# Batch 0's rows of v by one-hot matmuls in place of a gather, and the stores around the last gather in smaller parts, each waiting for one three or four places ahead

## The chip, the cores and the metric

The kernel runs on one core of a Trainium2 chip. The metric is the device time of one execution in microseconds (us), as the median of the runs shown. Engines are named as in the profile: PE (matmuls), DVE (vector), ACT (scalar), POOL (GpSimd, which here issues all loads, gathers and scatters on queue q0) and SP (which issues the stores on queue q1). Both queues are worked off by the same 16 DMA engines.

## What is computed

Four batches of q, k and v, each 6208 x 256 in float32. Attention runs across channels, so its matrix is 256 x 256, and a mixture-of-depths step then changes the 128 best rows of each batch:

```python
qn = q / (norm(q, axis=1) + 1e-06); kn = k / (norm(k, axis=1) + 1e-06)
s = kn.transpose(0, 2, 1) @ qn / tau
a = softmax(s)
x = v @ a                                   # (4, 6208, 256)
scores = x @ w_gate
for b in range(B):
    top_idx = the 128 rows with the highest scores[b]
    xe = x[b, top_idx]
    ye = np.maximum(xe @ w1, 0.0) @ w2      # w1 256 x 1024, w2 1024 x 256
    g = 1.0 / (1.0 + np.exp(-scores[b, top_idx]))
    out[b, top_idx] = xe + g[:, None] * ye
```

## The kernel before

A batch is cut into six chunks of 1024 rows and a rest of 64. A chunk's tile has 128 partitions with 8 rows each (RPP), so a full load moves 1 MB of float32 and casts it to 512 KB of bf16 on its way (emit_load, L187), and a store of a chunk sends 8 KB from each partition (emit_store, L514). The rest is a piece of its own and comes second in `order`.

For each batch the kernel goes through four stages. p1_row (L292) sums k'q and the squares of q and k on PE, row by row as the loads arrive. softmax_stages (L310) makes the 256 x 256 matrix a. p2_transpose (L392) turns v's tiles by PE into vt_sb, p2_score (L422) multiplies them with a's gate column for the scores, and p2_out (L456) multiplies them with a; ACT copies these outputs into a stage tile (L482). select_stages (L522) runs as a coroutine: seven rounds of compares and counts find the threshold (cmp, L557), a mask and its prefix counts give each chosen row its place (msk, pre), and idx, the 128 row numbers, follows (L622). Then POOL gathers the 128 rows of v from DRAM (L626) into vg; PE turns them (L637), DVE copies them to vgt (L639), and the small network runs on PE, ACT and DVE up to upd (L689). When the batch's stores have landed, POOL scatters upd over the output (L721).

The work is written out by a planner, while the program is built: a loop at the end of the kernel keeps a clock per engine (vt_clock) and a model of the two DMA queues (Rings), and at each step emits the ready piece of lowest priority number; each engine then runs its instructions in the order in which they were emitted. pump() issues the next load on POOL as soon as a buffer counts as free (in_use against limit) and fewer than four are in flight. out_store (L828) emits the stores on SP. Stores of batches 2 and 3 are deferred until the loads of the last batch are nearly done, and two chunks of batch 1 (`late`, with the change by the network applied in a matmul) go out last of all. SP and POOL work in order: a store or a load that waits holds all behind it.

```python
    QK_BUFS = 5
    V_BUFS = 5
    ST_BUFS = 9
    VT_BUFS = 11
...
        yield ("pool", 0.15, 0.9)
        vg = moe.tile([P, C], BF16, name="vg", bufs=2)
        ins = nc.gpsimd.indirect_dma_start(out=vg, out_offset=None, in_=v_flat,
                                     in_offset=bass.IndirectOffsetOnAxis(ap=idx[:, 0:1], axis=0))
```

Of the kernel before, what the change touches and what calls it, by code (L numbers as in the profile page):

```python
# [10 lines left out]
F32 = mybir.dt.float32  # L11
BF16 = mybir.dt.bfloat16
# [3 lines left out]
ALU = mybir.AluOpType  # L16
AX = mybir.AxisListType

P = 128
RPP = 8  # L20
CHUNK = RPP * P
NTHR = 8
# [5 lines left out]
def kernel(  # L28
# [12 lines left out]
    nc = tc.nc  # L41
# [13 lines left out]
    inv_tau = 1.0 / float(tau)  # L55

    QK_BUFS = 5
    V_BUFS = 5
    ST_BUFS = 9
    VT_BUFS = 11  # L60
    AHEAD = 4

    const = ctx.enter_context(tc.tile_pool(name="const", bufs=1))
# [88 lines left out]
    def now():  # L152
        return vt_clock["pe"]
# [110 lines left out]
    for i in range(NSTEP):  # L264
        nc.vector.memset(pows[:, i, :], 1.00001 / (NTHR + 1) ** (i + 1))
    jpows = const.tile([P, NSTEP, NTHR], F32)
    nc.vector.tensor_tensor(out=jpows, in0=pows,
                            in1=iota_row[:, None, 1:NTHR + 1].to_broadcast([P, NSTEP, NTHR]), op=ALU.mult)
    ones_col = const.tile([P, NCOL], BF16)
    nc.vector.memset(ones_col, 1.0)  # L270
    cnt9 = const.tile([P, NTHR + 1], F32)
# [219 lines left out]
    def emit_eights():  # L491
# [4 lines left out]
        for i in range(4):  # L496
# [3 lines left out]
            if i == 0:  # L500
# [2 lines left out]
                    mybir.DependencyInfo(mybir.DependencyClass.Sync, mybir.DependencyReason.DATA),  # L503
                    reason="stores behind loads")

    def emit_store(b, ci, parts):
        st = stage_of.pop((b, ci))
        ins = []
        keep = dmas if (b, ci) not in late else []
        if ci < NFULL:  # L510
            for h in range(parts):
                rows = slice(h * RPP // parts, (h + 1) * RPP // parts)
                low = slice(AHEAD_OF if (b, ci) == UNEVEN else 0, P)
                ins.append(nc.sync.dma_start(out=view(out, b, ci)[low, rows, :], in_=st[low, rows, :]))  # L514
        else:
            ins.append(nc.sync.dma_start(out=view(out, b, ci), in_=st[:REM, 0, :]))
        if (b, ci) not in late:
            held[b] -= 1
        keep.extend(ins)
        return ins[0]  # L520

    def select_stages(b):  # L522
        sc_ps = sc_tiles[b]
# [29 lines left out]
        nc.vector.tensor_scalar(out=tab, in0=jpows, scalar1=rng, scalar2=None, op0=ALU.mult)  # L553
        wait = 1.8
        for i in range(NSTEP):
            cmp = moe.tile([P, NCOL, NTHR], BF16, name="cmp", bufs=2)
            nc.vector.scalar_tensor_tensor(out=cmp, in0=sc[:, 0:NCOL, None].to_broadcast([P, NCOL, NTHR]),  # L557
                                           scalar=wl[:, i, NTHR:NTHR + 1],
                                           in1=tab[:, None, i, :].to_broadcast([P, NCOL, NTHR]),
# [39 lines left out]
        nc.tensor.matmul(sc_ps[:, 0, 0:1], lhsT=tri_b[:, 0, :], rhs=own_b, start=True, stop=True)  # L599
        excl_b = moe.tile([P, NCOL + 1], BF16, name="excl_b")  # L600
        nc.scalar.copy(excl_b, sc_ps[:, 0, 0:1].to_broadcast([P, NCOL + 1]))
        oh = moe.tile([P, P], BF16, name="oh")
        nc.vector.tensor_scalar(out=oh, in0=iota_row, scalar1=mps[:, 0:1], scalar2=None, op0=ALU.is_ge)
        nc.vector.scalar_tensor_tensor(out=oh, in0=iota_row, scalar=mps[:, 1:2], in1=oh, op0=ALU.is_lt,
# [13 lines left out]
        if b == late[0][0]:  # L618
# [2 lines left out]
        idx = moe.tile([P, 1], I32, name="idx", bufs=2)  # L621
        nc.vector.tensor_scalar(out=idx, in0=tok, scalar1=float(N - 1), scalar2=float(b * N), op0=ALU.min,  # L622
                                op1=ALU.add)
        yield ("pool", 0.15, 0.9)
        vg = moe.tile([P, C], BF16, name="vg", bufs=2)
        ins = nc.gpsimd.indirect_dma_start(out=vg, out_offset=None, in_=v_flat,  # L626
                                     in_offset=bass.IndirectOffsetOnAxis(ap=idx[:, 0:1], axis=0))
        dmas.append(ins)
        vt_clock["pool"] = max(vt_clock["pool"], now()) + 1.0
        rings.add(0, vt_clock["pool"] + 1.0, 0.5, ("gather", b))  # L630
        gathered.add(b)

        yield ("dma", ("gather", b))
        a_sb, _ = a_tiles[b]
        tp = ps_vt.tile([P, 2, 4, P], BF16, name="vt_ps")
        for cc in range(2):
            nc.tensor.transpose(tp[:, cc, 0, :], in_=vg[:, cc * P:(cc + 1) * P], identity=ident_b)  # L637
        vgt = moe.tile([P, 2, P], BF16, name="vgt")
        nc.vector.tensor_copy(vgt, tp[:, :, 0, :])  # L639
        yield ("pe", 0.12, 0.3)  # L640

        xt_ps = ps_vt.tile([P, 2, C], F32, name="vt_ps")
        for dc in range(2):
# [88 lines left out]
    def calm():  # L732

        if acc_dead[0]:
            return L in gathered
        if softmaxes[0]:
            return False
        near = eat[eat_at:eat_at + 14]
        return not any(x[0] == "T" for x in near) or near[0][0] == "T"

    class Chain:
# [33 lines left out]
        def ready(self):  # L775
            if self.need[0] == "t":
                if self.b == E and self.mlp and acc_dead[0] and L not in gathered:
                    return FAR
                return self.need[1]
            if self.need[0] == "dma":  # L780
# [12 lines left out]
            return max(rings.landing(key) for key in stored[b]) + 3.0  # L793
# [34 lines left out]
    def out_store(b, ci):  # L828
# [6 lines left out]
            gate = GATE  # L835
        if gate:
            vt_clock["sp"] = max(vt_clock["sp"], rings.landing(arrival_key[gate]))
        parts = 1 if ci == NFULL else 2 if b == L and ci in order[3:5] else 2 if 0 < len(gate_done) < 3 else 1
        if gate_done:
            gate_done.append(1)  # L840
        key = ("st", b, ci)
# [25 lines left out]
    while True:  # L867
# [106 lines left out]
        elif what == "T":  # L974
# [20 lines left out]
            vt_bank = sorted(vt_bank)[1:] + [fin]  # L995
            vt_live = len(from_pool)
            vt_ready[(u[1], g)] = fin
            if eat_at == len(eat) or eat[eat_at][1] != u:
                in_use[bucket(u)] -= 1
        elif what == "S":  # L1000
            b, g = scores[score_at]
# [61 lines left out]
```

## Time and profile before

| | us |
|---|---|
| median of 3 runs | 258.37 (258.06 to 258.6) |
| the profiled execution | 257.8 |
| its span | 255.8 |
| PE busy in the span | 214.7 |
| DVE busy | 92.6 |
| ACT busy | 106.4 |
| POOL busy | 56.9 |

The profile is that of one execution. Its span runs from the first to the last instruction; the execution's own time is 2.0 us longer. "Busy" of an engine is the time in which it ran an instruction. A DMA queue's share is the time that its packets took, as a share of 16 engines over the stretch; two queues can overlap, so that shares add up to a little over 100%. A strip shows the span (or a window) in 40 equal slices, each digit the busy share in tenths, 9 for 90% or more.

### The profile page before, as it was taken

The page shows a single profiled execution, that of the slowest core. Times are in us where ns is not written, and L with a number is a line of the kernel's source. Part 1 is how long each engine was busy: PE and PEld are TensorE (multiplying, and loading weights), DVE is VectorE, ACT ScalarE, POOL GpSimd, SP SyncE. Part 2 cuts the span into 40 slices and gives each one's busy share as a digit, 9 for nine tenths or more (in the row PEclk, how much of TensorE's full clock was granted, in tenths as well). Part 3 has the DMA queues.
Part 4 walks back from the last instruction along what each step waited for, and adds up shares of the span by engine and source line. Part 5 has one row for each costly group of instructions (what it writes and reads, how often), then busy time and mean ns, then how long its engine had stood idle before and what let it go on. Part 6 is the DMA issues. An engine that isn't in the chain of part 4 may idle for free.

```text
span 255.8 us, 6666 instructions
## 1 busy us (share of the span) xinstructions
PE 214.7 (84%) x2878; PEld 187.9 (73%) x2878; DVE 92.6 (36%) x410; ACT 106.4 (42%) x187; POOL 56.9 (22%) x106
## 2 busy tenths in 40 slices
PE   0099779899998529989999689899999999999962
PEld 0069768798877529879888578788898878887851
DVE  2000002635651003445655006546752064687021
ACT  2800003753564002484244005765313069698740
POOL 7323111422005000622200414212313310000301
PEclk9999999999999959999999999999999999999987
DMA  6999999999999999999999999999999999999995
GB/s 235 259 216 215 213 216 210 215 209 251 274 320 314 316 285 216 218 214 213 249 282 258 213 211 213 215 261 316 220 215 218 212 225 225 407 425 411 404 415 250
DMA packets 17326, 66.87 MB, mean 261 GB/s; under 512 B 2097, under 2 KB 3634, under 8 KB 14450
## 3 DMA queue, kind: packets, MB, share of 16 engines
q0 software_dynamic: 12672, 38.93, 76.5%
q1 hardware_dynamic: 4626, 27.53, 26.7%
q8 instruction: 22, 0.36, 0.5%
q14 instruction: 6, 0.05, 0.0%
HBM read 78.91 MB, written 25.95 MB: 410 GB/s over the span
## 4 chain that ended last, share of the span: by engine, by line
DMA 73%; PE 14%; issue 4%; POOL 4%; DVE 2%; ACT 1%; POOLq 1%; DVEq 0%
DMA k_ch<-in_k_dram 48%; DMA v_ch<-in_v_dram 10%; DMA q_ch<-in_q_dram 10%; DMA out_dram<-stage 4%; PE s_ps L303 2%; PE o_ps L474 2%; PE vt_ps L403 2%; POOL q_ch L187 1%; PE g_ps L307 1%; PE g_ps L305 1%; ACT stage L482 1%; PE s_ps L474 1%; PE sc_ps L440 1%; PE g_ps L474 1%; POOL k_ch L187 1%
## 5 line engine op out<-in xcount | busy, mean ns | idle before, releaser
L303 PE MATMUL s_ps<-q_ch,k_ch 128*128 128x256 bf16 x384 | 90.0, 279 | 28.7 <-DMA k_ch<-in_k_dram 28.7
L305 PE MATMUL g_ps<-q_ch 128*128 128x128 bf16 x384 | 85.5, 223 | 0.0
L307 PE MATMUL g_ps<-k_ch 128*128 128x128 bf16 x384 | 85.5, 223 | 0.0
L482 ACT COPY stage<-o_ps 128x512 f32<-128x512 f32 x77 | 43.9, 589 | 43.6 <-PE o_ps L474 41.6
L303 PEld LDWEIGHTS <-k_ch 128*128 128x128 bf16 x384 | 38.3, 100 | 31.5 <-DMA k_ch<-in_k_dram 30.6
L307 PEld LDWEIGHTS <-k_ch 128*128 128x128 bf16 x384 | 38.3, 100 | 5.2
L305 PEld LDWEIGHTS <-q_ch 128*128 128x128 bf16 x384 | 38.3, 100 | 0.1
L474 PE MATMUL o_ps<-a_sb,vt_sb 128*128 128x256 bf16 (+1 forms) x250 | 35.5, 272 | 1.0 <-ACT stage L482 0.5
L317 DVE CUSTOM_DVE_ANT_0 junk<-g_ps,ident_f 128x128 f32<-128x128 f32 x16 | 4.7, 291 | 66.4 <-PE g_ps L307 66.0
L474 PEld LDWEIGHTS <-vt_sb 128*128 128x128 bf16 (+1 forms) x264 | 23.6, 97 | 6.4 <-issue 3.1
L403 PE MATMUL vt_ps<-ident_b,v_ch 128*128 128x128 bf16 x360 | 25.4, 219 | 2.7 <-ACT vt_sb L417 2.4
L403 PEld LDWEIGHTS <-v_ch 128*128 128x128 bf16 x384 | 23.1, 97 | 5.1 <-issue 3.4
L313 ACT COPY s_sb<-s_ps 128x512 f32<-128x512 f32 x4 | 2.3, 586 | 55.4 <-PE s_ps L303 55.4
L187 POOL DMA_DIRECT2D v_ch<-in_v_dram x26 | 14.2, 545 | 45.8 <-PE vt_ps L403 17.5
L417 ACT COPY vt_sb<-vt_ps 128x1024 bf16<-128x1024 bf16 (+1 forms) x26 | 22.6, 927 | 2.9 <-PE vt_ps L403 2.9
L187 POOL DMA_DIRECT2D q_ch<-in_q_dram x25 | 13.8, 554 | 29.9 <-DMA q_ch<-in_q_dram 10.4
L187 POOL DMA_DIRECT2D k_ch<-in_k_dram x25 | 13.6, 543 | 24.5 <-DMA v_ch<-in_v_dram 10.4
L865 PE MATMUL o_ps<-w_sb,ident_b 128*128 128x256 bf16 x124 | 18.8, 273 | 0.2 <-ACT h_sb L675 0.2
L557 DVE SCALAR_TENSOR_TENSOR cmp<-sc,wl,tab 128x392 bf16<-128x392 f32 x28 | 17.5, 627 | 1.0
L626 POOL DMA_INDIRECT vg<-in_v_dram,idx x4 | 4.0, 1008 | 61.0 <-DVE idx L622 32.8
L865 PEld LDWEIGHTS <-ident_b 128*128 128x128 bf16 x124 | 10.7, 97 | 1.3 <-issue 0.4
L576 DVE TENSOR_REDUCE cnt<-m_ps 128x8 f32<-128x56 f32 x28 | 6.0, 216 | 15.3 <-PE m_ps L573 14.9
(188 smaller groups left out, 273.7 us busy)
## 6 DMA issues: line engine op xcount, KB each, us to landing
out_dram<-stage SPq DMA_DIRECT2D x21, 1024.0 KB, 10.2
q_ch<-in_q_dram POOLq DMA_DIRECT2D x23, 512.0 KB, 17.8
k_ch<-in_k_dram POOLq DMA_DIRECT2D x23, 512.0 KB, 18.5
v_ch<-in_v_dram POOLq DMA_DIRECT2D x22, 512.0 KB, 14.2
stage<-in_moe_w_dram SPq DMA_DIRECT2D x2, 1024.0 KB
out_dram<-stage SPq DMA_DIRECT2D x4, 512.0 KB
v_ch<-in_v_dram POOLq DMA_DIRECT2D x4, 256.0 KB, 12.9
out_dram<-stage SPq DMA_DIRECT2D x2, 384.0 KB, 5.0
```

The lines of the kernel that those rows point to most:

```text
L187: ins = nc.gpsimd.dma_start(out=t[:, rows, :], in_=view(src, b, ci)[:, rows, :])
L303: nc.tensor.matmul(s_ps[:, cc, :], lhsT=ks[:, sl], rhs=qs, start=begin and cc == 0, stop=end and cc == 1)
L305: nc.tensor.matmul(g_ps[:, cc, :], lhsT=qs[:, sl], rhs=qs[:, sl], start=begin and cc == 0, stop=False)
L307: nc.tensor.matmul(g_ps[:, 2 + cc, :], lhsT=ks[:, sl], rhs=ks[:, sl], start=False, stop=end and cc == 1)
L317: nc.vector.tensor_tensor_reduce(out=junk, in0=g_ps[:, i, :], in1=ident_f, scale=1.0, scalar=0.0, op0=ALU.mult, op1=ALU.add, accum_out=nsq ...
L403: nc.tensor.transpose(vt_ps[:, cc, j, :parts], in_=vt[:parts, s0 + j, cc * P:(cc + 1) * P], identity=ident_b[:parts, :parts])
L417: nc.scalar.copy(vt_sb[:, :, :n, :parts], vt_ps[:, :, :n, :parts])
L474: nc.tensor.matmul(o_ps[:parts, pj, :], lhsT=vt_sb[:, cc, j, :parts], rhs=a_sb[:, cc, :], start=pj == 0 and cc == 0, stop=pj == m - 1 and ...
L482: nc.scalar.copy(st[:parts, s0 + pair * 2:s0 + pair * 2 + m, :], o_ps[:parts, :m, :])
L557: nc.vector.scalar_tensor_tensor(out=cmp, in0=sc[:, 0:NCOL, None].to_broadcast([P, NCOL, NTHR]), scalar=wl[:, i, NTHR:NTHR + 1], in1=tab[: ...
L576: nc.vector.tensor_reduce(out=cnt9[:, 0:NTHR], in_=mps[:, 0:7 * NTHR].rearrange("p (s j) -> p j s", s=7), axis=AX.X, op=ALU.add)
L865: nc.tensor.matmul(o_ps[:, 0, :], lhsT=ident_b, rhs=w2_sb[:, 0, :], start=True, stop=True)
```

## The change

Batch 0 (`picked`) has no gather any more. Its tiles of v stay in SBUF until the choice is made: V_BUFS goes from 5 to 6, VT_BUFS from 11 to 8, and the planner does not count a tile of batch 0 as free after its transposes. DVE compares the place of each row (pos, 0 where it is not chosen) with the numbers 1 to 128 (place), four columns of rows at a time, in tiles that share the buffers of cmp. PE multiplies the tile of v with this one-hot matrix, 98 matmuls in all, which gives the chosen rows already turned; DVE copies them to vgt, and the network goes on as before. The other three batches gather as before (gathered_rows).

The stores of batch 3's chunks 1, 2 and 3 (order[2:5]) go in 2, 4 and 2 parts, where they went in 1, 2 and 2. Each part waits until an earlier store has landed: the planner goes back over the stores issued, adds up their time in its own model (2.46 for a chunk), and takes the first one that has more than 1.8 of stores between it and the part.

```diff
-    V_BUFS = 5
+    V_BUFS = 6
     ST_BUFS = 9
-    VT_BUFS = 11
+    VT_BUFS = 8
...
+    picked = (0,)
+
+    GRP = 4
+    place = const.tile([P, P], BF16)
+    nc.vector.tensor_scalar(out=place, in0=iota_row, scalar1=1.0, scalar2=None, op0=ALU.add)
...
                 ins.append(nc.sync.dma_start(out=view(out, b, ci)[low, rows, :], in_=st[low, rows, :]))
+                if b == L and ci in order[2:5]:
+
+                    ahead = 0.0
+                    for d, size in reversed(issued):
+                        if ahead > 1.8:
+                            tc.add_manual_dep(
+                                ins[-1].ins, d.ins.name,
+                                mybir.DependencyInfo(mybir.DependencyClass.Sync, mybir.DependencyReason.DATA),
+                                reason="a short queue")
+                            break
+                        ahead += size
+                issued.append((ins[-1], UNIT / parts))
...
+    def pick_rows(b, vp, g, pick):
+        for c in range(g, min(g + GRP, NCOL)):
+            ci, s = (c // RPP, c % RPP) if c < NCOL - 1 else (NFULL, 0)
+            parts = P if ci < NFULL else REM
+            vt = loaded[("v", b, ci)][0]
+            for cc in range(2):
+                nc.tensor.matmul(vp[:, 0, cc * P:(cc + 1) * P], lhsT=vt[:parts, s, cc * P:(cc + 1) * P],
+                                 rhs=pick[:parts, c - g, :], start=c == 0 and cc == 0,
+                                 stop=c == NCOL - 1 and cc == 1)
...
+        if b in picked:
+            pos = moe.tile([P, NCOL], BF16, name="pos")
+            nc.vector.scalar_tensor_tensor(out=pos, in0=pre[:, 0:NCOL], scalar=mps[:, 0:1], in1=msk,
+                                           op0=ALU.add, op1=ALU.mult)
...
+        if b in picked:
+
+            picks = []
+            for g in range(0, NCOL, GRP):
+                n = min(GRP, NCOL - g)
+                pick = moe.tile([P, GRP * P], BF16, name="cmp", bufs=2).rearrange("p (s t) -> p s t", t=P)
+                nc.vector.tensor_tensor(out=pick[:, 0:n, :], in0=pos[:, g:g + n, None].to_broadcast([P, n, P]),
+                                        in1=place[:, None, :].to_broadcast([P, n, P]), op=ALU.is_equal)
+                picks.append(pick)
+                if g == 0:
+                    yield ("pe", 0.0, 0.6)
+                    vp = ps_m.tile([P, 2, C], F32, name="m_ps")
+                    continue
+                pick_rows(b, vp, g - GRP, picks.pop(0))
+                if g % RPP == 0:
+                    in_use["v"] -= 1
+                yield ("pe", 0.46, 0.3)
+            pick_rows(b, vp, g, picks.pop(0))
+            vgt = moe.tile([P, 2, P], BF16, name="vgt")
+            nc.vector.tensor_copy(vgt, vp[:, 0, :].rearrange("p (a t) -> p a t", a=2))
...
-        parts = 1 if ci == NFULL else 2 if b == L and ci in order[3:5] else 2 if 0 < len(gate_done) < 3 else 1
+        parts = 1
+        if ci < NFULL and b == L and ci in order[2:5]:
+            parts = 4 if ci == order[3] else 2
+        elif ci < NFULL and 0 < len(gate_done) < 3:
+            parts = 2
...
-            if eat_at == len(eat) or eat[eat_at][1] != u:
+            if (eat_at == len(eat) or eat[eat_at][1] != u) and u[1] not in picked:
                 in_use[bucket(u)] -= 1
```

The order of the instructions shows where this lands. On POOL, in the loads of batch 1, the gather of batch 0 stood before the last pair of q and k loads:

```order
 L187 DMA q_ch<-in_q_dram 128x2048
 L187 DMA k_ch<-in_k_dram 128x2048
-L626 DMA vg<-in_v_dram,idx 128x256
 L187 DMA q_ch<-in_q_dram 128x2048
 L187 DMA k_ch<-in_k_dram 128x2048
```

Nothing takes its place; the loads close up. The first v load of batch 1 that follows now waits for PE, which reads batch 0's tiles.

On SP, the stores of batch 3 from its chunk 0 on, before the change. Stores take eight semaphores in turn (DMAHW0 to 7), and each waits for the last use of its own, eight stores back; Activation is ACT's copy into the stage:

```order
L514 DMA out_0_dram<-stage_3823 128x2048 [waits DMAHW3_49,Activation_49]
L516 DMA out_0_dram<-stage_rem_3864 64x256 [waits DMAHW4_49,Activation_49]
L514 DMA out_0_dram<-stage_3870 128x2048 [waits DMAHW5_49,Activation_49]
L514 DMA out_0_dram<-stage_3914 128x1024 [waits DMAHW6_49,Activation_49]
L514 DMA out_0_dram<-stage_3914 128x1024 [waits DMAHW7_49,Activation_49]
L514 DMA out_0_dram<-stage_4018 128x1024 [waits DMAHW0_49,Activation_49]
L514 DMA out_0_dram<-stage_4018 128x1024 [waits DMAHW1_49,Activation_49]
L514 DMA out_0_dram<-stage_4088 128x2048 [waits DMAHW2_49,Activation_49]
```

And now:

```order
L522 DMA out_0_dram<-stage_3910 128x2048 [waits DMAHW3_49,Activation_49]
L536 DMA out_0_dram<-stage_rem_3962 64x256 [waits DMAHW4_49,Activation_49]
L522 DMA out_0_dram<-stage_3968 128x1024 [waits DMAHW5_49,DMAHW2_49,Activation_49]
L522 DMA out_0_dram<-stage_3968 128x1024 [waits DMAHW6_49,Activation_49]
L522 DMA out_0_dram<-stage_4010 128x512 [waits DMAHW7_49,DMAHW3_49,Activation_49]
L522 DMA out_0_dram<-stage_4010 128x512 [waits DMAHW5_49,DMAHW0_49,Activation_49]
L522 DMA out_0_dram<-stage_4010 128x512 [waits DMAHW1_49,Activation_49]
L522 DMA out_0_dram<-stage_4010 128x512 [waits DMAHW6_49,Activation_49]
L522 DMA out_0_dram<-stage_4082 128x1024 [waits DMAHW7_49,Activation_49]
L522 DMA out_0_dram<-stage_4082 128x1024 [waits DMAHW4_49,DMAHW1_49,Activation_49]
L522 DMA out_0_dram<-stage_4161 128x2048 [waits Activation_49]
```

Chunk 1 (stage_3968) waits by DMAHW2 for batch 2's last chunk, the first quarter of chunk 2 (stage_4010) by DMAHW3 for chunk 0, the second and third by DMAHW5 for chunk 1's first half, the fourth by DMAHW6 for its second half, and chunk 3's halves by DMAHW7 and DMAHW1 for the first and third quarter. Chunk 4 (stage_4161) and those behind it have no such wait.

On DVE, batch 0's one-hot tiles stand right behind the index, with the rows of `cmp` as their buffers:

```order
L669 SCALAR_TENSOR_TENSOR tj,tok<-m_ps,iota_col,tj 128x50
L675 TENSOR_SCALAR idx<-tok 128x1
L683 TENSOR_TENSOR cmp<-pos,place 128x512 x12
L683 TENSOR_TENSOR cmp<-pos,place 128x128
L696 CAST vgt<-m_ps 128x256
L718 CAST xet<-vt_ps 128x256
```

On PE the 98 matmuls (L548) stand among the rows of batch 1's chunks 2 and 3, eight after every second row of k'q at most places.

## Rows read from the trace of the kernel before

**Rows 1.** The page: DMA busy share in 40 slices; instruction queue's packets, MB, share.
```profile
DMA  6999999999999999999999999999999999999995
q8 instruction: 22, 0.36, 0.5%
```

**Rows 2.** Windows: us, busy us per engine (instructions), clock, DMA share, GB/s.
```profile
12.00:60.00 48.00, 42.06 (x559) 36.76 (x560) 9.41 (x39) 13.44 (x24) 11.58 (x22) 1.00 1.07 213
80.00:100.00 20.00, 11.86 (x142) 10.63 (x140) 1.15 (x4) 1.98 (x5) 2.88 (x6) 0.83 1.06 288
215.00:237.00 22.00, 21.26 (x314) 17.85 (x312) 16.26 (x64) 17.84 (x38) 0.02 (x1) 1.00 1.02 394
```

**Rows 3.** The page, part 6: KB each, median us to landing.
```profile
k_ch<-in_k_dram POOLq DMA_DIRECT2D x23, 512.0 KB, 18.5
out_dram<-stage SPq DMA_DIRECT2D x21, 1024.0 KB, 10.2
```

**Rows 4.** Waits of POOL: total us, times, longest.
```profile
POOL vg L626 <- DVE idx L622: 32.8, 3, 17.4
```

**Rows 5.** Timeline of POOL: start, duration, instruction, idle before it.
```profile
78.54 1.02 POOL L626 DMA_INDIRECT vg<-in_v_dram,idx  x1 [17.38 <-DVE idx L622]
80.64 0.62 POOL L187 DMA_DIRECT2D v_ch<-in_v_dram  x1
```

**Rows 6.** DMA queues, 242 to 245 us: packets, MB, share of 16 engines.
```profile
q0 software_dynamic: 125, 0.07, 15.5%
```

**Rows 7.** DMA queues inside 242 to 246.6 us.
```profile
q1 hardware_dynamic: 255, 1.66, 88.5%
q0 software_dynamic: 188, 0.20, 17.6%
```

**Rows 8.** DMA queues, 222 to 233 us, 8 KB packets.
```profile
q1 hardware_dynamic: 635, 4.64, 100.9%
```

**Rows 9.** Groups of instructions (lines view), and a piece of the chain of waits.
```profile
L345 DVE TENSOR_TENSOR diag<-ident_f,rn 128x256 f32<-128x256 f32 x4 | 1.7, 425 | 0.1
42.72 0.91 PE vt_ps L403 x16
```

**Rows 10.** DMA queues, 239 to 242 us, 4 KB packets.
```profile
q1 hardware_dynamic: 323, 1.20, 101.4%
```

**Rows 11.** Timeline of SP: the first issue, and the last nine stores.
```profile
0.81 0.45 SPq L221 DMA_DIRECT2D stage<-in_moe_w_dram  x1
227.34 18.32 SPq L514 DMA_DIRECT2D out_dram<-stage  x9
```

**Rows 12.** DMA busy share in 40 slices of the first 7 us.
```profile
DMA  0000000000792219279999999999999979995999
```

**Rows 13.** View of the scatter's line L721, its last line.
```profile
DMA to landing us min/median/max: 2.9/2.9/2.9
```

**Rows 14.** Timeline from the last gather to the last scatter.
```profile
236.98 1.01 POOL L626 DMA_INDIRECT vg<-in_v_dram,idx  x1 [28.19 <-DMA out_dram<-stage]
244.72 0.58 ACT L482 COPY stage<-s_ps 128x512 f32<-128x512 f32 x1 [0.29 <-PE s_ps L479]
246.20 0.29 PE L637 MATMUL vt_ps<-ident_b,vg 128*128 128x128 bf16 x2 [1.52 <-DMA vg<-in_v_dram,idx]
251.13 0.48 DVE L689 SCALAR_TENSOR_TENSOR upd<-o_ps,gate,xe 128x256 f32<-128x256 f32 x1 [0.75 <-PE o_ps L684]
251.90 0.97 POOL L721 DMA_INDIRECT out_dram<-upd,idx  x1 [12.59 <-DMA out_dram<-stage]
```

**Rows 15.** End of the chain of waits: start, duration, what.
```profile
249.92 1.74 issue
```

**Rows 16.** DMA, 252 to 256 us: busy share in slices of 0.1 us.
```profile
DMA  9799574353131096953210000000000000000000
```

**Rows 17.** DMA queues, 253.4 to 254.4 us.
```profile
q0 software_dynamic: 47, 0.13, 34.5%
q1 hardware_dynamic: 7, 0.03, 7.9%
```

More of the change, by code (lines that the diff above doesn't have):

```diff
@@ L504, in emit_eights @@
                     reason="stores behind loads")
+    issued = []
     def emit_store(b, ci, parts):
@@ L520, in emit_store, with gathered_rows @@
         return ins[0]
+    def pick_rows(b, vp, g, pick):
[7 more added lines that the diff above has]
+                                 stop=c == NCOL - 1 and cc == 1)
+    def gathered_rows(b, idx):
+        vg = moe.tile([P, C], BF16, name="vg")
+        ins = nc.gpsimd.indirect_dma_start(out=vg, out_offset=None, in_=v_flat,
+                                           in_offset=bass.IndirectOffsetOnAxis(ap=idx[:, 0:1], axis=0))
+        dmas.append(ins)
+        vt_clock["pool"] = max(vt_clock["pool"], now()) + 1.0
+        rings.add(0, vt_clock["pool"] + 1.0, 0.5, ("gather", b))
+        gathered.add(b)
+        yield ("dma", ("gather", b))
+        tp = ps_vt.tile([P, 2, 4, P], BF16, name="vt_ps")
+        for cc in range(2):
+            nc.tensor.transpose(tp[:, cc, 0, :], in_=vg[:, cc * P:(cc + 1) * P], identity=ident_b)
+        vgt = moe.tile([P, 2, P], BF16, name="vgt")
+        nc.vector.tensor_copy(vgt, tp[:, :, 0, :])
+        yield ("pe", 0.12, 0.3)
+        return vgt
     def select_stages(b):
@@ L555, in select_stages @@
         for i in range(NSTEP):
-            cmp = moe.tile([P, NCOL, NTHR], BF16, name="cmp", bufs=2)
+            cmp = moe.tile([P, GRP * P], BF16, name="cmp", bufs=2)[:, 0:NCOL * NTHR].rearrange(
+                "p (s j) -> p s j", s=NCOL)
             nc.vector.scalar_tensor_tensor(out=cmp, in0=sc[:, 0:NCOL, None].to_broadcast([P, NCOL, NTHR]),
@@ L623, in select_stages @@
                                 op1=ALU.add)
[L624 to L633, printed above, removed]
-        a_sb, _ = a_tiles[b]
[L635 to L640, printed above, removed]
+        if b in picked:
[15 more added lines that the diff above has]
+            pick_rows(b, vp, g, picks.pop(0))
+            vgt = moe.tile([P, 2, P], BF16, name="vgt")
+            nc.vector.tensor_copy(vgt, vp[:, 0, :].rearrange("p (a t) -> p a t", a=2))
+            in_use["vr"] -= 1
+            yield ("pe", 0.1, 0.4)
+            yield ("calm",)
+        else:
+            yield ("pool", 0.15, 0.9)
+            vgt = yield from gathered_rows(b, idx)
+        a_sb, _ = a_tiles[b]
         xt_ps = ps_vt.tile([P, 2, C], F32, name="vt_ps")
@@ L779, in ready @@
                 return self.need[1]
+            if self.need[0] == "calm":
+                return now() if calm() else FAR
             if self.need[0] == "dma":
```

## The prediction

> **What bounds the kernel now.** I read the busy strip first. The DMA engines stand at 9 from the second slice to the last but one [rows 1]: the kernel is bound by the work laid on the 16 DMA engines. The windows give the rate of each mix [rows 2]: loads alone 213 GB/s (counted as the bf16 written; twice that is read), loads beside stores 288, stores nearly alone 394, the DMA share above 1 in all of them. The compute engines wait: from 80 to 100 us PE is busy 11.86 of 20 us and DVE 1.15. The queues are deep: a k load lands 18.5 us after its issue in the median, a 1 MB store 10.2 us [rows 3]. So an issue that comes some microseconds sooner or later leaves no hole. The time can change in three ways only: work taken off or put on the DMA engines, a hole where a queue runs dry, and the last two microseconds, where the engines run out one by one.
>
> This settles what looks like the largest item. POOL waits 32.8 us in three places for the index of a gather, 17.4 us of it for batch 0's [rows 4], and until 78.54 the loads behind stand still [rows 5]. The change takes this wait away, but the strip shows 9 throughout it (from 61 to 78 us, slices of 6.4 us). I price it at nothing: the loads and stores already queued cover it.
>
> **The change part by part.**
>
> *Batch 0's gather goes.* The nearest rows are those of the last gather. From 242 to 245 us queue q0 holds little else: 125 packets, 15.5% of 3 us, 0.47 us of all engines [rows 6]. The rest of the gather follows until 246.6 us; with it I estimate 0.55 us, the upper end. Two queues overlap a little, though: from 242 to 246.6 us q0 took 17.6% (0.81 us) while the stores had 88.5% [rows 7] where they have 100.9% alone [rows 8], 12.4% of 4.6 us, 0.57 us. So 0.7 of a packet's time is paid, 0.33 us for the 0.47, the lower end. I take the middle, **-0.42 us**.
>
> *What replaces it.* DVE makes 12 one-hot tiles of 512 columns and one of 128. The nearest row, a two-operand DVE operation of 256 columns, takes 425 ns [rows 9]; twice that bounds a tile, 12 x 0.85 + 0.25 = 10.5 us. PE gets 98 matmuls of 128 columns, at 0.91/16 = 0.057 us each 5.6 us [rows 9]. They stand where batch 0's index was ready, 78.5 us, and the window from 80 to 100 has 18.9 us of DVE and 8.1 us of PE free [rows 2]. Cost 0, hidden by the loads that PE waits for there; without this cover it would be up to 10.5 us. Batch 0's tiles of v are held longer: the first is free after the second group, 78.5 + 2 x 0.85 + 0.5 = 80.7 us, and the first v load of batch 1 went at 80.64 us before [rows 5]. With k's 18.5 us of queue, cost 0. Eight buffers of transposed v in place of eleven put some transposes behind output matmuls on PE, the gathers of batches 1 and 2 stand one v load later on POOL, and batch 1's scatter one pair of loads sooner; the same queue hides these.
>
> *Smaller stores.* Batch 3's chunk 1 goes from 8 KB to 4 KB packets, chunk 2 from 4 KB to 2 KB, chunk 3 keeps 4 KB. In 8 KB packets 4.64 MB left in 11 us [rows 8], 2.49 us for a chunk of 1.05 MB; in 4 KB packets 1.20 MB in 3 us [rows 10], 2.62 us. So chunk 1 pays 0.13 us for 8 more packets per engine, and chunk 2 with 16 more 0.27 us, 0.40 us in all. The lower end is 0 (the window of 4 KB packets is short; the same bytes in more packets cannot gain); the upper end doubles the step to 2 KB, which no row shows: 0.67 us. I take **+0.35 us**, near the measured pair.
>
> *The waits on SP.* Six stores (chunk 1's first, three quarters of chunk 2, both halves of chunk 3) wait until the store three or four places ahead has landed. Behind them on SP stand all later stores; POOL's last scatter waits for batch 3's. Before, SP issued nine in the 18.3 us from 227.34 [rows 11] as soon as ScalarE had the rows, so the waits bind. When a wait ends, 0.62 + 1.24 = 1.87 us of stores are still queued (at 2.49 us a chunk). What must fit inside is the way from release to first packet: the program's first SP issue at 0.81 us [rows 11] made the engines busy in slice 10 of 0.175 us, by 1.75 to 1.93 us [rows 12], so 0.9 to 1.1 us. That leaves 0.8 us to spare, and a wait can only delay. The upper bound is the last scatter, alone: 2.9 us to landing [rows 13] less 0.97 us of POOL, 1.93 us, which would be 6 x (1.93 - 1.87) = 0.4 us of holes. I take **0**, the row of the same queue.
>
> The Trainium skill (DMA: Bandwidth & Descriptors, section Anatomy of one DMA) speaks against this part: a DMA has about 2.0 us of fixed cost, mostly the receipt of the last write, so a chain of waits pays it at each link. By that rule 2.0 - 1.87 = 0.13 us is lost six times and the sum would be 0.8 us higher, an estimate from that page; no run here shows it yet.
>
> *The last gather and the end.* It is issued at 236.98 and first used at 246.20 us; PE's late outputs end just before the copy at 244.72 us; then 4.9 us to the update at 251.13 and the scatter at 251.90 us [rows 14]. With at most about 3 us of small stores queued it lands before PE is free, so this chain starts near 244.6 and the scatter goes about 1.6 us sooner, at 250.3 us, just after batch 3's stores landed, 249.92 us [rows 15]. What is it worth? From 252.4 us the strip falls to 5, 7, 4, 3 and comes up again to 9 when the scatter's packets arrive [rows 16]. But at 253.4 to 254.4 us the stores still hold 7.9% beside the scatter's 34.5% [rows 17]: a few engines are still at their stores. On these the scatter's share now comes ahead of the last store instead of behind it, which is the same work. Only the overlap of two queues is gained, 0.3 x 0.345 = **-0.10 us**; the ends are 0 and the even finish below, -1.0 us.
>
> *Instruction fetch.* the order shows 205 more instructions on PE and DVE; 6666 came in 22 packets, so that is one more, and the 22 took 0.5% of 255.8 us [rows 1], 1.3 us: **+0.06 us**.
>
> Sum: -0.42 + 0.35 + 0 - 0.10 + 0.06 = -0.11 us. The profiled execution took 257.8 us (span 255.8 us and 2.0 us around it), 0.6 us under the median of the runs, 258.37; the sum gives 257.7 against it and 258.26 against the median. I predict **258.2 us**, no change that can be told (0.2% is 0.52 us, about what a measurement here can tell). With the ends of the terms this case runs from 257.6 to 258.8 us.
>
> **The rivals.**
>
> *Faster, by the end.* If the engines still at their stores after 253.4 us are behind only because the gather and scatter came late, the early scatter fills the holes. From 252.4 us the strip's digits add up to 67 tenths of 0.1 us [rows 16], 0.67 us of work, spread over 1.7 us; finished evenly it would end 1.0 us sooner. With -0.42, +0.35 and +0.06 that is -1.0 us: 257.3 us. For it speaks the strip, against it the 7.9%. Chance 0.27.
>
> *Slower, by dry waits.* On SP at chunk 2's quarters the queue may run out before the released store's packets arrive, if a wait ends only with the last of the 16 engines, and the engines do not end together [rows 16]. It decides from 1.87 us between landing and first packet on; at 2.1 us six waits lose 6 x 0.2 = 1.2 us: 259.5 us. This is the page's rule as a mechanism of this kernel. Against it: 1.1 us on the same queue. Chance 0.13.
>
> *Slower, by held tiles.* POOL's loads stand in order behind batch 1's v loads, which now wait for PE to read batch 0's tiles. If the groups go at 1.3 us instead of 0.85, the last tile is free at 95 instead of 89 us and the load queue may empty; 1.5 us lost gives 259.8 us. Against it: 18.5 us of queue. Chance 0.05.
>
> That the change does not do what it says is hardly open: the order of the instructions shows the gather gone and the waits in place.
>
> **How the numbers follow.** Forecast 0.55, the three rivals 0.27, 0.13 and 0.05. Faster by over 0.2% (below 257.85) is the first rival and a small part of the forecast, 0.30; slower (above 258.89) the other two, 0.18; the rest, 0.52, within. The range takes in the forecast's ends, the first rival's 257.3 and half of the slower ones: 257.2 to 259.2 us, leaving out about 0.1 on each side.
>
> **What would show it.** Right: the strip at 9 up to the last slice with no dip near 60 to 100 us; one gather fewer; the last gather landing before 244.7 us and the last scatter issued near 250.3 us; stores of 239 to 245 us no faster than 400 GB/s; the DMA running out at the same 254 us. Wrong: a strip below 9 between 233 and 243 us (dry waits) or between 85 and 106 us (held tiles); a DMA that ends evenly near 253 us (first rival).

## The result: slower by 0.67%, and the profile after

The changed kernel takes 259.83 us in the median of 22 runs (258.92 to 263.05), the kernel before 258.51 us in 22 runs beside it (257.74 to 259.45). The ratio is 1.0067 with a 95% interval of 1.0048 to 1.0086: slower by 1.7 us. The prediction said 258.2 us and no change; it was wrong, and the result lies outside its range. The profiled execution took 259.57 us, its span 257.9 us, 2.1 us more than before. All ratios here leave out the executions that took over 1.5% more than the fastest of their kernel: one of the changed kernel's, one in experiment 4 and three of nine in experiment 7.

The page of the changed kernel, parts 2 and 3 (the strip in 40 slices of 6.4 us, then the queues as packets, MB, share):

```profile
DMA  6999999999999999999999999999999999997995
GB/s 235 261 216 215 212 214 212 215 210 281 291 316 317 315 239 214 223 214 221 291 285 214 214 210 214 215 307 277 214 224 207 214 228 285 421 419 315 325 430 238
...
q0 software_dynamic: 12528, 38.87, 75.6%
q1 hardware_dynamic: 5058, 27.53, 26.6%
q8 instruction: 23, 0.38, 0.5%
```

The strip of before had 9 throughout [rows 1]. Now one slice falls to 7, and two have 315 and 325 GB/s between neighbours of 419 and 430: 232 to 245 us, where the stores wait. Nothing else in the busy strip moved, and the instruction queue has the one packet more that was expected.

The same stretch closer, DMA queues from 230 to 246 us, slices of 0.4 us, first after, then before:

```profile
DMA  9999999969899999539515999999989689999999
...
q1 hardware_dynamic: 1506, 5.19, 84.1%
q0 software_dynamic: 192, 0.20, 6.6%
```

```profile
DMA  8989999999999999999999999999999999999999
...
q1 hardware_dynamic: 1226, 6.31, 97.1%
q0 software_dynamic: 169, 0.16, 4.5%
```

Both queues together had 101.6% of 16 us, now 90.7%: 10.9% of 16 us, 1.7 us of the 16 engines are gone, and 1.08 MB less was written and gathered. At the end this comes out again. DMA from 252 to 259 us, slices of 0.175 us, first after, then before:

```profile
DMA  8989998998989888651210000000000100000000
```

```profile
DMA  7965343196410000000000010000000000000000
```

Before, the engines ran out in the twelfth slice, 254.0 us; now in the twenty-first, 255.6 us.

The last gather did what the change wants of it, though from a worse start. Timeline of POOL, PE and DVE after (start, duration, instruction, idle before it), to be held against [rows 14]:

```profile
239.12 1.00 POOL L554 DMA_INDIRECT vg<-in_v_dram,idx  x1 [32.82 <-PE o_ps L485]
...
244.85 0.28 PE L564 MATMUL vt_ps<-ident_b,vg 128*128 128x128 bf16 x2
...
248.43 0.48 DVE L752 SCALAR_TENSOR_TENSOR upd<-o_ps,gate,xe 128x256 f32<-128x256 f32 x1 [0.23 <-PE o_ps L747]
...
252.01 0.97 POOL L784 DMA_INDIRECT out_dram<-upd,idx  x1 [10.60 <-DMA out_dram<-stage]
```

It is issued at 239.12 us, 2.1 us later than before, and still landed by 244.85, where PE takes it without idle time; the update is made 2.7 us sooner (248.43 for 251.13). Half of the 2.7 us is the earlier gather; the other half is the small network, 3.6 us from its first matmul to the update where it took 4.9. PE's granted clock was 1.00 (2.4 GHz) from 246 to 249 us; before it was 0.50 (1.2 GHz) from 248 to 250 us, after PE had been busy for 1.69 us of the three from 243 us and had stood idle for 1.52 us until the gather landed.

But the scatter goes no sooner (252.01 for 251.90). Before, it followed the end of the update (251.61 us) by 0.29 us; the row in [rows 14] names a store, but batch 3's stores had all landed 2 us earlier. Now it stands 3.1 us behind the update and waits for these stores. The last of them in the chain of waits (start, duration, what), first before, then after:

```profile
238.50 11.03 DMA out_dram<-stage
```

```profile
242.04 9.06 DMA out_dram<-stage
```

It landed at 249.53 us before (the prediction's 249.92 is the end of POOL's waits behind it) and lands at 251.10 us now, 1.6 us later. So two things were to be explained, the holes and the late gather.

### The profile page after: what moved, and what is told of

It is laid out like the page before. It is cut to its first block, busy times and chain, and to the rows that moved or that the text cites. A ratio compares the mean times of both kernels' runs of the same rounds, so it can differ in the third digit from the quotient of the medians.

```text
span 257.9 us, 6916 instructions
## 1 busy us (share of the span) xinstructions
PE 216.9 (84%) x2972; PEld 191.2 (74%) x2972; DVE 103.7 (40%) x428; ACT 103.6 (40%) x184; POOL 55.7 (22%) x105
## 4 chain that ended last, share of the span: by engine, by line
PE 47%; DMA 34%; ACT 6%; DVE 5%; issue 4%; POOL 2%; POOLq 1%; DVEq 0%; ACTq 0%
DMA k_ch<-in_k_dram 21%; DMA out_dram<-stage 9%; PE o_ps L480 8%; PE s_ps L309 8%; PE vt_ps L409 6%; DMA q_ch<-in_q_dram 4%; PE g_ps L313 4%; PE g_ps L311 4%; PE o_ps L934 4%; PE sc_ps L446 3%; PE m_ps L548 2%; ACT e L363 2%; ACT stage L488 2%; ACT vt_sb L423 1%; PE g_ps L480 1%
## 5 line engine op out<-in xcount | busy, mean ns | idle before, releaser
L488 ACT COPY stage<-o_ps 128x512 f32<-128x512 f32 x77 | 44.0, 590 | 40.6 <-PE o_ps L480 38.3
L423 ACT COPY vt_sb<-vt_ps 128x1024 bf16<-128x1024 bf16 (+1 forms) x24 | 20.9, 922 | 1.6 <-PE vt_ps L409 1.6
L934 PE MATMUL o_ps<-w_sb,ident_b 128*128 128x256 bf16 x122 | 17.1, 273 | 0.2 <-ACT h_sb L738 0.2
L425 DVE COPY vt_sb<-vt_ps 128x1024 bf16<-128x1024 bf16 x11 | 7.6, 691 | 14.4 <-PE vt_ps L409 14.3
L554 POOL DMA_INDIRECT vg<-in_v_dram,idx x3 | 3.0, 999 | 45.2 <-PE o_ps L485 32.8
## 6 DMA issues: line engine op xcount, KB each, us to landing
v_ch<-in_v_dram POOLq DMA_DIRECT2D x4, 256.0 KB, 12.6
out_dram<-stage SPq DMA_DIRECT2D x4, 256.0 KB
```

The lines of the kernel that those rows point to most:

```text
L423: nc.scalar.copy(vt_sb[:, :, :n, :parts], vt_ps[:, :, :n, :parts])
L425: nc.vector.tensor_copy(vt_sb[:, :, :n, :parts], vt_ps[:, :, :n, :parts])
L488: nc.scalar.copy(st[:parts, s0 + pair * 2:s0 + pair * 2 + m, :], o_ps[:parts, :m, :])
L934: nc.tensor.matmul(o_ps[:, 0, :], lhsT=ident_b, rhs=w2_sb[:, 0, :], start=True, stop=True)
```

## The experiments

The first four expectations name theories by letters; the main one, A, is that the dry waits are the whole loss, against the smaller packets (B) and batch 0's held tiles of v (C). The ratios in all of them are against the kernel before on the same chip, with the 95% interval. Each profile shows one execution; that of experiments 1, 2, 8 and 11 was the shortest of its run.

**1. The change without its waits.** The edit:

```diff
-                if b == L and ci in order[2:5]:
+                if False:
                     ahead = 0.0
```

> The change without its six waits on SP; the parts (2, 4, 2) and the one-hot matmuls stay. Dry waits (theory A): the holes of 233 to 239 us in the strip are the whole loss, so they close and the time falls from 1.0067 of the kernel before to 1.000 or a little under, 258.0 to 258.6 us. Packet size (rival B): 2 KB packets keep their price without the waits, 259.3 us or more. Held tiles (rival C): the loss sits in the loads, 259.5 us or more.

Measured: 1.0093 [1.0068, 1.0119]. Without the waits there are no holes, and the kernel is no faster. Theory A, as the whole loss, falls. The DMA strip of this run from 252 to 259 us and the last scatter show where the time is now:

```profile
DMA  9899885341403110000000099100000000000000
```

```profile
254.49 0.98 POOL L784 DMA_INDIRECT out_dram<-upd,idx  x1 [12.44 <-DVE upd L752]
```

The stores run out at 254.5 us, the engines stand still, and at 256.0 us come the scatter's packets alone: the scatter waits for `upd`, as before the change, and not for a store.

**2. The one-hot matmuls alone**: no waits, and the stores in the parts of before.

> The one-hot matmuls alone: stores in the parts of the kernel before, no waits. Theory A: a gather's 0.3 to 0.5 us less on the DMA engines and nothing else, ratio 0.998 to 0.9995. Rival B (packets): the same as A here. Rival C (held tiles): 1.004 or more, the loss is all here.

Measured: 1.012 [1.0092, 1.0149]. So neither the waits nor the parts make this loss; theory C has the number right here, and experiment 8 tells whether for its reason. Its timeline of POOL, PE and DVE:

```profile
239.45 1.00 POOL L554 DMA_INDIRECT vg<-in_v_dram,idx  x1 [32.73 <-DMA out_dram<-stage]
...
249.05 0.36 PE L564 MATMUL vt_ps<-ident_b,vg 128*128 128x128 bf16 x2 [3.72 <-DMA vg<-in_v_dram,idx]
...
253.68 0.48 DVE L752 SCALAR_TENSOR_TENSOR upd<-o_ps,gate,xe 128x256 f32<-128x256 f32 x1 [0.23 <-PE o_ps L747]
...
254.45 0.98 POOL L784 DMA_INDIRECT out_dram<-upd,idx  x1 [12.69 <-DMA out_dram<-stage]
```

The gather goes 2.5 us later than before, and behind a full queue of stores it is used 9.6 us after its issue (before 9.2). PE idles 3.7 us for it, and the scatter goes at 254.45 us, 2.5 us later than before. Its row names a store, but it stands 0.29 us behind the end of the update (254.16 us) as in experiment 1, and the chain of waits has batch 3's last store landed at 250.02 us: the update releases it. From there the kernel has 3.5 us left, as in experiment 1.

**3. The stores alone**: the kernel before, with the parts and the six waits of the change.

> The kernel before with the parts and the six waits alone, batch 0 gathers as before. Theory A: the whole loss and the gather's saving missing, ratio 1.007 to 1.009. Rival B: the same. Rival C: 1.000.

Measured: 1.0046 [1.0027, 1.0065], below the 1.007 to 1.009 of theories A and B, above C's 1.000. The choice is early here (gather at 237.61 us), and what is left is the holes. DMA from 230 to 246 us in this run:

```profile
DMA  9999979999875999999993796956999999999998
```

**4. The change with `ahead > 4.0`** in place of 1.8, a longer queue behind each wait.

> The change with more than 4.0 instead of 1.8 of stores (in the planner's own time) between a part and the store it waits for. Theory A: a landing plus the way to the next first packet, with engines about 2 us apart, is under 4 us, so no engine runs dry: as e1, 1.000 or under. Rival B: no change from the changed kernel, 1.006. A rival D, that any wait on a landing costs by itself, says 1.004 or more.

Measured: 1.006 [1.0034, 1.0087]. No holes (queue q1 at 99.4% from 230 to 246 us), the gather issued at 239.63, the scatter at 255.15 us: as experiment 1. Theory A falls here too. (Theory D, that any wait on a landing costs by itself, fits this number; experiment 10, with waits and 1.000, goes against it.) By now the theory was: two costs. The version with the one-hot matmuls makes batch 3's choice late, and behind a full queue this late gather ends the kernel; the waits shorten the queue, which in the trace takes much of that back (the gather used 5.7 us after its issue in place of 9.3 in experiment 1, the scatter 2.5 us sooner), and cost holes. By time alone this isn't shown: the intervals of the change and of experiment 1 overlap.

**5. What makes the choice late: the buffers alone.** The kernel before with

```diff
-    V_BUFS = 5
+    V_BUFS = 6
-    VT_BUFS = 11
+    VT_BUFS = 8
```

> The kernel before with the change's buffers alone: V_BUFS 6 in place of 5, VT_BUFS 8 in place of 11. Batch 0 gathers as before, no waits, the stores as before. Theory now (late choice): with eight buffers of transposed v, batch 2's output matmuls have to free tiles before batch 3's transposes can be written, so batch 3's scores end 2 us later, the last gather is issued 2 to 2.8 us later behind a deep queue of stores, and the scatter ends the kernel; the plan for batch 3 is the same here as in the version with the one-hot matmuls alone, so the ratio is 1.008 to 1.013, scores ending near 222.7 us (before 220.7), the gather issued after 239 us. Rival (the one-hot matmuls themselves do it, by their time on PE and DVE or by held tiles of v): 0.999 to 1.002, the gather near 237 us.

Measured: 1.0113 [1.0077, 1.0149], as much as experiment 2 with the one-hot matmuls in it. The gather goes at 240.02 us, the scatter at 256.39 us. How eight buffers do it is seen on PE between the exponentials of batch 3 and its scores. Timeline of PE before, and after:

```profile
209.18 0.60 PE L474 MATMUL o_ps<-a_sb,vt_sb 128*128 128x256 bf16 x4
209.62 0.61 PE L403 MATMUL g_ps<-ident_b,v_ch 128*128 128x128 bf16 x8
210.06 0.61 PE L403 MATMUL vt_ps<-ident_b,v_ch 128*128 128x128 bf16 x8
210.51 0.82 PE L865 MATMUL o_ps<-w_sb,ident_b 128*128 128x256 bf16 x6
211.17 0.61 PE L403 MATMUL s_ps<-ident_b,v_ch 128*128 128x128 bf16 x8
211.61 0.61 PE L403 MATMUL vt_ps<-ident_b,v_ch 128*128 128x128 bf16 x8
212.49 0.54 PE L440 MATMUL sc_ps<-aw_sb,q_ch 128*128 128x2 bf16 x16 [0.26 <-DVE aw_sb L371]
```

```profile
208.73 0.60 PE L480 MATMUL o_ps<-a_sb,vt_sb 128*128 128x256 bf16 x4
209.16 0.60 PE L480 MATMUL g_ps<-a_sb,vt_sb 128*128 128x256 bf16 x4
209.60 0.61 PE L409 MATMUL vt_ps<-ident_b,v_ch 128*128 128x128 bf16 x8
210.05 0.60 PE L480 MATMUL s_ps<-a_sb,vt_sb 128*128 128x256 bf16 x4
210.49 0.60 PE L480 MATMUL o_ps<-a_sb,vt_sb 128*128 128x256 bf16 x4
211.55 0.61 PE L409 MATMUL g_ps<-ident_b,v_ch 128*128 128x128 bf16 x8 [0.47 <-ACT stage L488]
211.99 0.61 PE L409 MATMUL vt_ps<-ident_b,v_ch 128*128 128x128 bf16 x8
212.95 0.61 PE L409 MATMUL s_ps<-ident_b,v_ch 128*128 128x128 bf16 x8 [0.35 <-ACT stage L488]
213.40 0.54 PE L446 MATMUL sc_ps<-aw_sb,q_ch 128*128 128x2 bf16 x16
```

Before, one group of batch 2's output matmuls (a_sb,vt_sb) stands there, beside filler of L865, and PE then waits for aw_sb: the scores start the moment they can. After, four such groups have to come first, to free tiles of transposed v for batch 3's transposes; these in turn wait twice for ACT, which has the outputs' copies to make. aw_sb was ready sooner than before (started at 211.81 for 212.27 us), yet the scores start 0.9 us later (213.40 for 212.49) and have their last row 1.65 us later (222.01 for 220.36). `idx` follows 1.6 us later (238.19 for 236.55), the gather 2.1 us. PE of experiment 5 itself has the same order, with the four groups and the same two waits for ACT (0.47 and 0.35 us). The half microsecond between `idx` and the gather is not the buffers': the gather starts 0.93 to 0.94 us after `idx` in the change and in experiments 2 and 8, and 0.43 us before the change and in experiment 5. The new code takes `vg` with one buffer in place of two, and POOL has a wait of its own ahead of that gather; whether the one makes the other was not tried.

**6. The price of a gather.** The kernel before with

```diff
-        ins = nc.gpsimd.indirect_dma_start(out=vg, ...
+        if b == 0:
+            nc.vector.memset(vg, 0.0)
+        else:
+            ins = nc.gpsimd.indirect_dma_start(out=vg, ...
```

> The kernel before without batch 0's gather: its tile is filled with zeros by DVE, all else in the plan stays. Left out: batch 0's chosen rows are not read from v. It prices the term of the prediction for the gather, -0.42 us: 0.998 to 0.999 by the prediction, with the bounds -0.33 to -0.55 us. Rival (the gather's packets cost nothing that the DMA engines do not get back, or POOL's wait for the index counts after all): 0.9995 to 1.0005. Whoever holds that the change's loss is all in the end needs this to be 1.000 or below.

Measured: 0.9993 [0.9974, 1.0011]. Inconclusive: both expectations lie in the interval.

**7. The change with `ahead > 2.8`.**

> The change with 2.8 in place of 1.8 in the rule for the waits, so each waits for a store a place or so further ahead. Theory now (two costs that are traded): fewer holes in the strip at 233 to 240 us (under 0.5 us of them in place of 1.6), the last gather landing 5.5 to 7.5 us after its issue in place of 5.5; the scatter issued at 252 to 253.5 us; the ratio between 1.003 and 1.008, no better than 1.002 because the choice is as late as in the change. Rival (the holes are the whole loss): 1.000 or below.

Measured: 1.0043 [1.0007, 1.0079]. The holes are nearly gone (q1 at 97.7% from 230 to 246 us), the scatter waits to 254.77 us, later than expected, and the gather is used 8.4 us after its issue. Removing the holes does not bring the time back while the choice is late; its rival falls, by a small margin (1.0007 for 1.000).

**8. The one-hot matmuls with room**: as experiment 2, but with the eleven buffers of before. The room comes from the stage and from leaving out `place`:

```diff
-    ST_BUFS = 9
-    VT_BUFS = 8
+    ST_BUFS = 8
+    VT_BUFS = 11
...
+            nc.vector.tensor_scalar(out=pos, in0=pos, scalar1=-1.0, scalar2=None, op0=ALU.add)
...
-                                        in1=place[:, None, :].to_broadcast([P, n, P]), op=ALU.is_equal)
+                                        in1=iota_row[:, None, :].to_broadcast([P, n, P]), op=ALU.is_equal)
```

> The one-hot matmuls alone, without the waits and with the stores as before, but with all eleven buffers of transposed v: the room comes from a stage tile less (ST_BUFS 8 in place of 9) and from comparing with the row of numbers 0 to 127 itself, one small DVE operation more. Theory now (late choice by eight buffers): batch 3's part of the plan is as in the kernel before, the scores end near 220.7 us, the last gather is issued near 237 us, and the loss of 1.2% is gone: 0.998 to 1.002. Rival (the one-hot matmuls or the held tiles of v delay the rest): 1.008 to 1.013. If the stage tile that is missing costs something, it shows as SP or ACT waiting for a stage between 100 and 200 us, and the ratio may reach 1.005.

Measured: 1.0005 [0.9982, 1.0027]. The loss of 1.2% is gone with the one-hot matmuls still there. Its timeline of PE and POOL:

```profile
211.71 0.54 PE L444 MATMUL sc_ps<-aw_sb,q_ch 128*128 128x2 bf16 x16 [0.23 <-DVE aw_sb L375]
...
236.80 1.00 POOL L552 DMA_INDIRECT vg<-in_v_dram,idx  x1 [30.74 <-PE o_ps L478]
...
250.58 0.97 POOL L783 DMA_INDIRECT out_dram<-upd,idx  x1 [11.47 <-DMA out_dram<-stage]
```

The scores again start when aw_sb is there, the gather goes at 236.80 us, and the scatter at 250.58 us, held by the stores and no longer by the update, which is done at 250.17. With experiment 5, which loses as much by the buffers alone, this makes eight buffers the cause (the stage tile less shows no cost of its own), and the one-hot matmuls and the tiles that they hold are none; theory C falls.

**9. The whole change with room**: experiment 8 with the parts and the waits at 1.8.

> The whole change (one-hot matmuls, parts, waits at 1.8) with eleven buffers of transposed v, the room made as in the run of the one-hot matmuls with room. Theory (the loss of the change is two costs: a late choice by eight buffers, which the short queue of stores partly takes back, and holes by the waits): the choice is as early as before, the gather is issued near 237 us and lands within 5.5 us, and the holes alone are left, as where the stores were changed alone: 1.003 to 1.007, holes of 1 to 2 us between 233 and 241 us, stores landing last near 255.9 us. Rival (the two do not add up because the buffers matter with the waits too): 1.007 or above. Rival (with early picks and waits the early gather brings what the change is for): 1.000 or below.

Measured: 1.0037 [1.0015, 1.0059]. The choice is early, the holes are left (q1 at 78.1% from 230 to 246 us), and they cost what they cost in experiment 3.

**10. The same with `ahead > 2.8`.**

> As the run of the whole change with room, with 2.8 in place of 1.8 in the rule for the waits: each waits for a store further ahead. Theory: the holes shrink to under 0.5 us, the gather is issued near 237 us and lands after 6 to 8 us, the DMA work is that of the kernel before, so 0.999 to 1.003. If an early gather can buy anything at the end, this is the best place for it: below 0.998. Rival (smaller parts cost by themselves): 1.002 to 1.004 without holes in the strip.

Measured: 1.000 [0.998, 1.0021]. q1 keeps 94.6% from 230 to 246 us. The end of this run, PE and POOL, and the DMA strip from 252 to 259 us:

```profile
243.96 0.28 PE L562 MATMUL vt_ps<-ident_b,vg 128*128 128x128 bf16 x2
...
250.35 0.98 POOL L783 DMA_INDIRECT out_dram<-upd,idx  x1 [11.13 <-DMA out_dram<-stage]
```

```profile
DMA  7967954211010000000000100000000000000000
```

This is the change as it was meant: gather early, no wait on it, scatter 1.5 us sooner than before (251.90), the DMA out at the same 254 us. It buys nothing that can be told: from the scatter to the end of the span pass 5.9 us here and 3.9 before, and the DMA engines finish no sooner: the stores end the kernel then. No version tried here beats the kernel before while it does the whole work.

**11. The parts alone**: the kernel before with 2, 4 and 2 parts, no waits.

> The kernel before with the change's smaller stores alone (chunks 1, 2 and 3 of batch 3 in 2, 4 and 2 parts), without the waits and with the buffers and gathers of before. The prediction put +0.35 us on this (bounds 0 and 0.67): 1.0014, at most 1.0026. Theory now: the run of the whole change with room and a middle queue stood at 1.000 with the same parts, so the parts cost next to nothing: 0.9995 to 1.001. Rival (the parts are the larger share of what the stores cost, and the holes the smaller): 1.003 to 1.005.

Measured: 0.9996 [0.9977, 1.0016]. The parts cost nothing that shows, and theory B falls as the cause of the loss. The prediction's 1.0014 is still inside the interval, its upper end, 1.0026, is not.

**12. Three gathers left out**, experiment 6 with `if b < L:`.

> The kernel before without the gathers of batches 0, 1 and 2: their tiles are filled with zeros by DVE, the plan stays. Left out: the chosen rows of three batches are not read from v. It trebles the price that one gather's run left between -0.2% and 0: by the prediction's -0.42 us each the ratio is 0.9951 (bounds 0.9936 to 0.9962). Rival (the packets of a gather among loads cost the DMA engines next to nothing, since the rest of the stream runs the faster): 0.9985 to 1.0005.

Measured: 0.9953 [0.9928, 0.9978]. The profile of this run was taken on its longest execution (259.61 us; the median is 257.83), so no line is read from it. A third of 0.47% is 0.16%, 0.41 us for a gather, with 0.19 to 0.62 as bounds. POOL's waits for the three indices (32.8 us before, [rows 4]) go away with the gathers, so the price is that of a gather and its wait together; no run parts them.

## Why the prediction was wrong, step by step

*What bounds the kernel now* held up: holes and the last microseconds are where the runs that lost did so, and work taken off the DMA engines is where experiment 12 gained. But the sentence "an issue that comes some microseconds sooner or later leaves no hole" was carried from the deep queue of before to a stretch in which the change cuts the queue short.

***The waits on SP*, taken at 0, failed.** The step said that 1.87 us of stores are still queued when a wait ends, and that 0.9 to 1.1 us pass from release to first packet. The second half came out at 0.8 to 0.9 us, near enough; the first is wrong. SP's waits after, and two of its issues:

```profile
SPq L522 <- DMA out_dram<-stage: 11.0, 6, 6.4
```

```profile
236.26 0.33 SPq L522 DMA_DIRECT2D out_dram<-stage  x1
...
237.73 0.33 SPq L522 DMA_DIRECT2D out_dram<-stage  x1
```

And the DMA engines from 237 to 240 us, slices of 0.075 us:

```profile
DMA  0689896899712020100017999999989999999898
```

The second quarter of chunk 2 is released and issued at 237.73 us. The engines had come down to 1 or 2 tenths in the twelfth slice, from 237.8 us on, and its packets fill them from the twenty-second, 238.6 us: 0.8 to 0.9 us after the issue. So not 1.87 us were left in the queue, but about 0.1. The reason is what the second rival named: a wait ends with the last of the 16 engines. In the trace's records of that store (chunk 1's first half) the first engine is done at 235.40 us, the middle one at 235.87 and the last at 237.66, just ahead of the release; the 1.87 us that the step counts on go by while one engine is waited for. The first quarter's wait, for chunk 0, went the same way (middle 234.32, last 236.21, issued at 236.26 us) and made the hole before. Over the six waits the last engine lands 0.3 to 1.9 us after the middle one. The mechanism and its point of decision (1.87 us) stood in the prediction, with the price 1.2 us; the stores alone lose 1.0046 x 258.5 - 258.5 = 1.2 us (0.7 to 1.7). That the two prices agree is luck: the rival had six equal holes of 0.2 us, the strip of the change shows two large ones, at 236.4 to 237.2 and 237.6 to 238.8 us, and that of experiment 3 holes of several sizes. That its 259.5 us for the whole change is near the measured 259.83 is luck too, since the buffers have a part in that. What was wrong is the choice between two bounds: I took the way of one packet from an idle start [rows 11, 12] as the nearest row, though it tells nothing of how a landing is reported, and gave the rival 0.13. Rows of the same store's engines would have told: the strip of [rows 16] already showed engines that end far apart.

The Trainium skill (DMA: Bandwidth & Descriptors, section Anatomy of one DMA) gives about 2.0 us of fixed cost for a DMA that POOL issues, mostly the last write's receipt; carried over to SP's stores, the loss was to be 0.8 us, an estimate. The run of the stores alone agrees with the sign and, within its interval, with the size, but the trace shows another cause: the spread of the engines, 1.8 us from the middle one to the last.

***What replaces it*, taken at 0, failed in one clause**: "Eight buffers of transposed v in place of eleven put some transposes behind output matmuls on PE ... the same queue hides these." The queue of stores hides nothing here; it is what the late gather has to go through. Alone this costs 1.1% (experiment 5), 2.9 us. The delay on PE is in the order of the instructions, and I priced it by the loads it could hold up, not by batch 3's scores, which stand ahead of the last gather, the update and the scatter. The rest of that step was right where it counts: a one-hot tile took 659 ns in the mean (bounded at 850), 96 of PE's matmuls took 7.1 us (estimated 5.6 for 98), and though the first v load of batch 1 waits until 84.06 us (estimated 80.7, before 80.64 [rows 5]), the strip from 60 to 106 us has 9 throughout. The *held tiles* rival fell with that.

**The two errors do not add up.** Holes alone +0.46%, late choice alone +1.1 to 1.2%, both +0.67%. With the short queue the late gather lands in 5.5 us instead of being used 9.2 to 10.1 us after its issue, and is off the end again; then the holes are paid, and about 0.3% on top of experiment 9's 0.37%, which is no more than the two intervals together leave open.

*Batch 0's gather goes*, -0.42 us: borne out for the gather and its wait together (0.41 us by experiment 12, 0.19 to 0.62); that the middle agrees so well is luck. Whether the one-hot matmuls give something of it back stays open: experiment 8 stands at 1.0005, and its lower bound of 0.9982 just reaches the -0.16%.

*Smaller stores*, +0.35 us: not shown. Experiment 11 has -0.04% with 0.2% either way, nearest to the lower end, 0, with 0.35 us still inside.

*The last gather and the end*, -0.10 us: not met in the change, where the scatter went at 252.01 us for the 250.3 forecast (the 4.9 us that this step gave the network were those of the halved clock; at full clock it took 3.6); but where holes and late choice are taken away (experiment 10) it goes at 250.35 us, and the gain is indeed too small to see. The *faster by the end* rival, the likeliest of the three at 0.27, has this run against it: an early scatter did not shorten the DMA's end. *Instruction fetch* had its one packet right; its price no run shows.

## What to carry to other kernels

A wait for a DMA ends with its slowest engine, not when its bytes are through on average: a chain of waits that keeps a queue short needs, beyond the issue's own way, the spread of the engines as reserve, here 1.8 us more (with over 2.8 us of stores, in the planner's count, behind each wait it stayed nearly full, with over 1.8 it did not). When a change pays for itself with buffers of another stage, look in the new order of the instructions for what those buffers let run early, and follow it to the last step of the kernel: here a cut from 11 to 8 cost 2.9 us, where the gather that it made room to replace cost some 0.4. And a gather that comes earlier is worth nothing where the stores that it runs beside end at the same time anyway.

## What the runs showed of the hardware

The 16 engines leave the same store up to 2.3 us apart (235.40 to 237.66 us). An indirect gather of 128 rows behind a full queue of stores was used 9.2 to 10.1 us after its issue (before and experiments 1, 2, 5 and 8); with the queue cut short by waits it landed 4.3 to 5.5 us after (the change and experiments 3, 9 and 10). PE's granted clock was at half while the last network ran in the kernel before (0.50 from 248 to 250 us) and in experiment 2 (0.50 from 250 to 252 us), each time after PE had waited for the gather, 1.52 and 3.72 us; in experiment 8 it waited 2.11 us and kept 1.00. And packets of half the size cost little. From 237 to 240 us, most of them the 2 KB packets of the change:

```profile
q1 hardware_dynamic: 436, 0.83, 72.4%
```

72.4% of 16 x 3 us are 34.8 us of the engines' time for 0.83 MB, 41.9 us for a MB; in 4 KB packets it was 101.4% for 1.20 MB [rows 10], 40.6 us for a MB, about 3% less.
